# Moving the low parts of decoded weights and the division of the probabilities from GpSimd to VectorE

## The chip, the cores and the metric

The kernel runs on one core of one Trainium2 chip. The metric is the time of one execution on the device in microseconds (us). The profile comes from one execution of the same program under the hardware profiler. The core's engines work side by side, each through its own queue in order: TensorE (PE; PEld is its weight load), VectorE (DVE), ScalarE (ACT), GpSimd (POOL) and SyncE (SP), which here issues most of the DMAs.

## The reference, cut to what matters

Three layers follow each other on 2304 tokens of width 512.

```python
# 1. attention with a window of 64 keys: 4 batches, 8 heads, 576 positions, head width 64
scores = where(mask, scale * q @ k.T, -1e9)
attn = exp(scores - scores.max(-1))
attn = attn / (attn.sum(-1) + 1e-9)          # the division of the probabilities
x = attn @ v                                  # -> [2304, 512]
# 2. gated layer, w_a and w_b 512 x 1536, w_out 1536 x 512
x = ((x @ w_a) * (x @ w_b)) @ w_out
# 3. soft mixture of 8 experts with 4 slots each
logits = x @ phi                              # softmax over the tokens and over the slots
out = softmax(logits, 1) @ experts(softmax(logits, 0).T @ x)
```

The inputs are float32 for the attention and float64 for some weights: w_a, w_b and w_out arrive as pairs of 32-bit words, and the kernel makes float32 of them on the chip ("decoding").

## The kernel before, in words

The tokens are worked through in 18 tiles of 128. For each tile the attention is computed, then the products with w_a and w_b in three column groups (fg) of 512, then their product with w_out times phi, and running softmax sums. The products with w_a and w_b are made in two precisions: a weight is split into a high part, rounded to the fast matmul format, and a low part, the rest; each 128-deep step makes three matmuls (line 430): high x high, high x low, low x high.

All of w_a and w_b has to be decoded and split first: 24 pieces of 128x512, named by matrix, column group and depth, such as Da0.3 or Db2.1. One piece goes through seven steps: ScalarE takes the absolute value (line 365); VectorE clamps (367), shifts (369), sets the top bits (373) and the bottom bits (377); ScalarE rounds the high part (413); and the low part is the difference of the two (415). The difference is made by GpSimd. The decoded float32 piece lies in one of four buffers that are used in turn (tags gT0 and gT1), and a buffer is free for a later piece only when the difference is made. The 12 pieces of w_out (Po0 to Po11) go through the same decode steps in the same four buffers; their st buffers come from a pool of three, which late pieces of w_b use too, and they have no difference.

The attention of a tile has, on VectorE, the masking with its row extremes (line 271), the sums plus epsilon (290) and their reciprocal (292), and then the multiplication of the probabilities by it (296): in tiles 0 to 4 by GpSimd, in later tiles by VectorE. The transposes of the probabilities on TensorE wait for it.

The order of the work at the beginning is written out by hand: the string STARTUP is a list of steps, and the program advances the named piece of work by one step each time its name stands there. This fixes the order of every engine's queue and of the DMA issues (SyncE's, and GpSimd's for wo); an engine goes on to its next instruction as soon as that one's own inputs are there, so the queues may stand at different places of the list at the same time. Names are: Tq, Tv loads of q, k and v; Aq, Ak, As, An, Ap, Av the steps of the attention of a tile; Sa, Sb loads of a piece of w_a or w_b; Da, Db its seven steps; Ga, Gb the gated layer's matmuls of a tile and column group, with the copy (437) or product (439) at their end; Po a piece of w_out; Rt transposes; Ri constants; Ph the load of phi. Behind the list, only TensorE's order is written by hand.

Of the kernel before, what the change touches and what calls it, by code (L numbers as in the profile page):

```python
# [22 lines left out]
STARTUP = """
    Ak0 Tq0 Aq0 Tq0 Sb0.0 Aq0 Sa0.2 Db0.0 Ak0 Sb0.2 Db0.0 Ak0 As0 Da0.2 As0 Da0.2 Tq1 Db0.0 Db0.2 Db0.0 Tq1
    Sa0.0 Sa0.1 Aq1 As0 As0 Tq2 Db0.0 As0 Db0.0 Ak1 Da0.2 Db0.0 An0.0 An0.0 Ak1 Aq1 Ak1 As0 Da0.2 Db0.2 Db0.2
    As1 Db0.2 Da0.0 Db0.2 An0.1 As1 Ak2 Da0.2 Da0.0 An0.0 As1 Da0.0 Tq2 Db0.2 Da0.2 Da0.1 Sb0.1 Aq2 As1 Da0.2
    An0.1 Ap0.0 Da0.0 Da0.0 Sb0.3 Aq2 Tv0 Db0.1 Ak2 An0.1 Ap0.0 Da0.1 Db0.2 Ap0.1 Db0.3 Da0.0 An1.0 An1.0 Ak2
    Db0.1 Db0.1 Da0.1 As1 Tv0 Ap0.1 Av0 As1 Db0.1 Tq3 As2 Da0.1 Av0 Db0.1 As2 Da0.1 An1.1 An1.1 Db0.1 Ak3 Av0
    Db0.3 Sa0.3 Da0.1 As2 Da0.0 An1.0 Aq3 Da0.3 Tq3 Sa1.0 Gb0.0 Sa1.1 Da0.3 Ap1.0 An1.1 Da0.3 Tv1 Tv1 Aq3 Da0.1
    Ga0.0 Db0.3 As2 Da0.3 Ap1.0 Ak3 Db0.3 Ga0.0 Tq4 Ak3 Sb1.0 Ga0.0 Db0.1 Da0.3 Ap1.1 Da1.0 Da1.1 An2.0 As2 As3  # L30
    Db0.3 Da1.1 Da1.1 As3 Da0.3 Db0.3 Gb0.0 Da1.0 Ap1.1 Sa1.2 Av1 Sa1.3 Da0.3 As2 Da1.0 Av1 Gb0.0 Da1.1 An2.0
    Db0.3 Da1.0 An2.1 Da1.0 Ga0.0 Ga0.0 An2.1 Gb0.0 Da1.1 An2.0 Av1 Gb0.0 Tq4 Ap2.0 As3 Db1.0 Da1.0 Ga1.0 Aq4
    Gb1.0 Ak4 Po1 Da1.2 Db1.0 Ga1.0 Ga1.0 Da1.0 Ap2.0 Gb1.0 Db1.0 Da1.1 Tv2 Da1.3 Gb1.0 Da1.2 Ak4 As3 Sb1.1 Tv2
    Db1.0 Da1.1 Aq4 Da1.2 An2.1 Ak4 Ga1.0 Sb1.2 Da1.3 Da1.2 Db1.0 Da1.3 Sb1.3 Ga1.0 Da1.2 As3 Gb1.0 Da1.2 Da1.3
    Ap2.1 Po1 An3.0 Po1 Da1.2 Da1.3 Db1.0 Ga0.1 Db1.0 Po1 Ap2.1 As4 Ga0.1 Po4 Po1 Ga0.1 As4 Po1 Gb1.0 Da1.3
    Db1.1 As3 As4 Da1.3 Db1.2 Po1 An3.0 Db1.1 Db1.1 An3.0 Db1.2 Ga0.1 Tv3 Ga0.1 Db1.1 Po1 Po3 Db1.3 Db1.2 Po1
    Db1.1 Db1.1 Ph0 Db1.3 Db1.2 Av2 Gb0.1 Sa2.0 Sa2.1 Ga1.1 Av2 Po4 Ga1.1 Db1.2 Po4 Av2 An3.1 Po4 Db1.3 Ga1.1
    An3.1 Db1.3 Ga1.1 Db1.1 Ga1.1 Ap3.0 Db1.2 Tv3 Gb0.1 Ga2.0 Ga2.0 Ga2.0 As4 Db1.2 Po3 Ga2.0 As4 Da2.0 Ga2.0
    Po1 An3.1 Db1.3 Po3 Sa2.2 Po4 Ap3.1 An4.0 Db1.3 As4 Db1.3 Da2.0 Gb0.1 Ga2.1 Po3 An4.0 Po7 Po4 Po3 Ga2.1 Po3
    Po4 Ga2.1 Po3 Gb0.1 Gb0.1 Ap3.0 Po4 Ga2.1 Da2.1 Da2.1 Ap3.1 Da2.1 Av3 Gb2.0 Po3 Gb2.0 Da2.0 Po1 Tv4 Av3  # L40
    Da2.1 Sa2.3 Gb2.0 Gb2.0 Ri0 Tq5 Po1 Sb2.2 Ga2.1 Av3 Da2.0 Ga3.0 Da2.1 Da2.0 Po0 Ga3.0 Da2.2 Gb2.0 Da2.0
    Da2.2 An4.0 Po4 Po3 Gb1.1 Po1 Da2.0 Da2.2 Sb2.0 Gb1.1 Tv4 Da2.1 Gb1.1 Ga3.0 Po5 Da2.3 Da2.2 Po7 Ga3.0 Da2.2
    Po7 Da2.3 Gb1.1 Po7 Da2.2 Po4 An4.1 Tq5 Da2.1 Da2.2 Ga3.0 Po7 Da2.3 An4.1 Gb1.1 Po0 Da2.3 Po7 Ap4.0 Ga0.2
    Gb2.1 Po4 Ga0.2 Da2.3 Db2.0 Da2.3 Po4 Sb2.1 Db2.0 Po7 Da2.3 Po0 Ap4.0 Po5 Gb2.1 An4.1 Po4 Gb2.1 Gb2.1 Ga0.2
    Db2.0 Po0 Ga0.2 Po3 Po7 Po0 Db2.0 Po0 Ga0.2 Po6 Po5 Db2.0 Po5 Ga1.2 Po3 Ga1.2 Po3 Po5 Po7 Po5 Po0 Db2.1
    Gb2.1 Ga1.2 Po2 Db2.0 Po5 Db2.1 Po0 Po5 Po3 Db2.2 Db2.2 Db2.1 Po7 Po7 Gb3.0 Ga1.2 Db2.0 Ga1.2 Db2.2 Gb3.0
    Po2 Po7 Db2.1 Gb3.0 Po0 Db2.2 Ga3.1 Db2.1 Po5 Gb3.0 Po6 Ga3.1 Sb2.3 Po7 Po2 Gb3.0 Po5 Po5 Ga3.1 Db2.2 Po2
    Po6 Db2.1 Db2.2 Po2 Po2 Po6 Ga3.1 Ap4.1 Ga3.1 Db2.1 Po6 Po6 Po2 Db2.3 Gb3.1 Ga2.2 Po5 Gb3.1 Gb3.1 Po5 Po8
    Po0 Db2.2 Ak5 Gb3.1 Db2.3 Po9 Db2.3 Po0 Db2.3 Po0 Ak5 Ga2.2 Po6 Po0 Gb3.1 Ap4.1 Po8 Ga2.2 Po2 Ak5 Gb0.2
    Db2.3 Av4 Po8 Po8 Po8 Po2 Po2 Ga2.2 Po8 Db2.3 Gb0.2 Po11 Db2.3 Po2 Gb0.2 Po6 Tv5 Po2 Po10 Gb0.2 Ga2.2 Tv5  # L50
    Po2 Po8 Po9 Gb0.2 Po6 Ga3.2 Po6 Po11 Gb1.2 Po6 Ga3.2 Po9 Po8 Gb1.2 Ga3.2 Po6 Po11 Po9 Po8 Po10 Po10 Gb1.2
    Po9 Po6 Po8 Gb1.2 Rt0.0 Po9 Po8 Gb1.2 Ga3.2 Po9 Po9 Rt0.0 Aq5 Po9 Po8 Po11 Po10 Av4 Po11 Po8 Po11 Gb3.2
    Gb3.2 Aq5 Po11 Po10 Po9 Ga3.2 Po11 Po9 Po10 Po10 Gb3.2 Po11 Po10 Po9 Rt0.2 Po9 Po10 Gb3.2 Rt0.2 Rt0.1 Gb3.2
# [968 lines left out]
```

## Time and profile before

| what | value |
|---|---|
| median of 3 runs | 539.0 us (538.02 to 540.81) |
| the profiled execution, its own time | 537.18 us |
| its span, first to last instruction | 535.4 us |
| TensorE, share of the span | 92% |
| VectorE | 59% |
| ScalarE | 38% |
| GpSimd | 23% |
| HBM traffic | 215 GB/s over the span |
| mean granted TensorE clock | 0.991 of full speed |

The profiled execution is 1.8 us longer than its span (start and end around the first and last instruction). The shares are means over the whole span. The list STARTUP covers about the first 140 us.

### The profile page before, as it was taken

To read this page: it belongs to the slowest core of one execution; us is meant where nothing else is said; L and a number is where in the kernel's file an instruction comes from. 1 tells how busy PE (TensorE), PEld (TensorE's weight loads), DVE (VectorE), ACT (ScalarE), POOL (GpSimd) and SP (SyncE) were. 2 spreads that over 40 slices of the span, in tenths; PEclk is the share of its full clock that TensorE was granted. 3 is DMA by queue.
4 is the path that set the end of the run, shared out by engine and by line. 5 is a ranking of instruction groups with operands and counts; after the bars stand their busy time and mean duration, and the time that the engine had idled before them with its cause. 6 is when DMAs were issued, how large, how long until landed. Compare 5 with 4: busy or idle time off the path is not lost.

```text
span 535.4 us, 10977 instructions
## 1 busy us (share of the span) xinstructions
PE 492.5 (92%) x4039; PEld 362.4 (68%) x4039; DVE 315.1 (59%) x897; ACT 201.3 (38%) x621; POOL 120.7 (23%) x182
## 2 busy tenths in 40 slices
PE   4479788899998999999999999999999999989992
PEld 3367566677776777787778787787777777743452
DVE  3999999896456474756647466377674211242132
ACT  5667575354444232433324233243432212141012
POOL 3555447532000212112031120313221000020000
PEclk9998999999999999999999999999999999999997
DMA  9987168647444759776676657767779899799997
GB/s 275 259 240 240 44 224 249 204 146 203 119 119 104 199 129 239 192 184 156 159 190 145 179 142 174 197 159 180 190 213 291 305 360 366 265 343 341 348 350 245
DMA packets 142102, 116.01 MB, mean 217 GB/s; under 512 B 81888, under 2 KB 122848, under 8 KB 142048
## 3 DMA queue, kind: packets, MB, share of 16 engines
q1 hardware_dynamic: 136864, 99.58, 63.6%
q0 software_dynamic: 5184, 15.73, 10.4%
q8 instruction: 32, 0.52, 0.4%
q14 instruction: 22, 0.18, 0.1%
HBM read 90.90 MB, written 24.38 MB: 215 GB/s over the span
## 4 chain that ended last, share of the span: by engine, by line
PE 74%; DVE 15%; DMA 4%; issue 3%; ACT 1%; SPq 1%; POOL 0%; POOLq 0%; ACTq 0%
PE psb L430 25%; PE psa L430 24%; PE ops L924 3%; PE xps L346 3%; PE ups L558 3%; PE lps L482 3%; DVE w L373 3%; PE h L890 2%; PE s L258 2%; DVE w L377 2%; DVE w L367 2%; DVE pr L271 2%; PE tg L138 1%; DVE w L369 1%; DMA st<-in_moe_w_b_dram 1%
## 5 line engine op out<-in xcount | busy, mean ns | idle before, releaser
L430 PE MATMUL psb<-whb,x 128*128 128x512 f32 x432 | 153.7, 407 | 2.8 <-DVE g L439 2.2
L430 PE MATMUL psa<-wha,x 128*128 128x512 f32 x432 | 152.0, 406 | 2.4 <-ACT wha L413 1.6
L430 PEld LDWEIGHTS psb<-whb,x 128*128 128x128 f32 x432 | 81.3, 188 | 30.3 <-issue 9.9
L430 PEld LDWEIGHTS psa<-wha,x 128*128 128x128 f32 x432 | 81.1, 188 | 24.1 <-issue 3.9
L430 PE MATMUL psa<-wla,x 128*128 128x512 f32 x216 | 84.5, 391 | 1.0 <-POOL wla L415 1.0
L430 PE MATMUL psb<-wlb,x 128*128 128x512 f32 x216 | 84.6, 391 | 0.9 <-POOL wlb L415 0.9
L439 DVE TENSOR_TENSOR g<-psb,g 128x512 f32<-128x512 f32 x53 | 36.5, 689 | 71.5 <-PE psb L430 68.6
L437 ACT COPY g<-psa 128x512 f32<-128x512 f32 x53 | 31.1, 586 | 92.9 <-PE psa L430 82.6
L278 ACT ACTIVATE pr<-pr,nmx 128x128 f32<-128x128 f32 x144 | 56.0, 393 | 17.7 <-DVE nmx L271 17.7
L312 POOL DMA_DIRECT2D pd<-pq x48 | 26.4, 557 | 116.8 <-DVE pq L305 86.3
L430 PEld LDWEIGHTS psa<-wla,x 128*128 128x128 f32 x216 | 40.7, 189 | 8.3 <-POOL wla L415 1.4
L430 PEld LDWEIGHTS psb<-wlb,x 128*128 128x128 f32 x216 | 40.7, 189 | 7.6 <-POOL wlb L415 1.2
L349 ACT CAST x<-xps 128x512 fp32r<-128x512 f32 x18 | 10.6, 587 | 51.3 <-PE xps L346 51.3
L258 PE MATMUL s<-kTs,qTs 64*64 64x128 f32 x576 | 23.5, 299 | 6.4 <-DVE nmx L271 3.5
L457 DVE STREAM_TRANSPOSE gq<-g 128x512 f32<-128x512 f32 x39 | 27.4, 705 | 1.2 <-DMA gd<-gq 0.6
L278 ACT ACTIVATION_READ_ACCUMULATOR pr<-pr,nmx 128x1 f32 x144 | 27.4, 190 | 0.0
L318 POOL DMA_DIRECT2D pT<-pd x24 | 18.1, 758 | 39.9 <-DMA pd<-pq 35.4
L271 DVE CUSTOM_DVE_ANT_0 pr<-s,masks 128x128 f32<-128x128 f32 x112 | 24.8, 285 | 3.3 <-PE s L258 3.3
L258 PEld LDWEIGHTS s<-kTs,qTs 64*64 64x64 f32 x576 | 18.1, 147 | 10.1 <-issue 4.7
L232 POOL COPY kTs<-kTs 128x256 f32<-128x256 f32 x17 | 8.2, 483 | 66.1 <-DVE kTs L243 61.4
L415 POOL TENSOR_TENSOR wlb<-w,whb 128x512 fp32r<-128x512 f32 x12 | 17.5, 1455 | 18.4 <-ACT whb L413 18.4
L367 DVE TENSOR_SCALAR w<-w 128x512 f32<-128x512 f32 x24 | 14.4, 602 | 10.2 <-ACT w L365 10.2
(140 smaller groups left out, 721.8 us busy)
## 6 DMA issues: line engine op xcount, KB each, us to landing
xw<-in_moe_w_dram SPq DMA_DIRECT2D x39, 512.0 KB, 6.9
xw<-in_moe_w_dram SPq DMA_DIRECT2D x50, 256.0 KB, 5.9
gd<-gq SPq DMA_DIRECT2D x156, 64.0 KB, 2.9
gT<-gd SPq DMA_DIRECT2D x39, 256.0 KB, 3.2
st<-in_moe_w_b_dram SPq DMA_DIRECT2D x12, 512.0 KB, 5.9
st<-in_moe_w_a_dram SPq DMA_DIRECT2D x12, 512.0 KB, 5.5
st<-in_moe_w_out_dram SPq DMA_DIRECT2D x12, 512.0 KB, 5.2
pd<-pq POOLq DMA_DIRECT2D x48, 128.0 KB, 3.1
```

What stands on the lines that cost most here:

```text
L258: nc.tensor.matmul(sps[h][c, u], lhsT=qT[r, u, c], rhs=kTs[r, t % 2, u, W * b:W * b + P],)
L271: nc.vector.tensor_tensor_reduce(out=pr[:, u].rearrange("p (a k) -> p a k", a=2), in0=sps[h][:, u].rearrange("p (a k) -> p a k", a=2), in1 ...
L278: nc.scalar.activation(out=pr[:, u], in_=pr[:, u], func=ACTF.Exp, scale=-1.0, bias=nmx[:, i:i + 1], accum_out=sm[:, i:i + 1],)
L312: nc.gpsimd.dma_start(out=pd[:, :, i].rearrange("j k e -> k j e"), in_=pq[32 * i:32 * i + 32].rearrange("p j h u q -> p j (h u q)"),)
L318: nc.gpsimd.dma_start(out=pT, in_=pd[:, :, :, P * h:P * h + P].rearrange("j k i e -> (j k) i e"))
L346: nc.tensor.matmul(o, lhsT=vt[:, 2 * u + h, :], rhs=r)
L367: nc.vector.tensor_scalar(out=t, in0=t, scalar1=DBL_LO, scalar2=DBL_HI, op0=ALU.max, op1=ALU.min)
L415: nc.gpsimd.tensor_tensor(out=lo, in0=w32, in1=hi.bitcast(F32), op=ALU.subtract)
L430: nc.tensor.matmul(ps, lhsT=l[:, kk], rhs=r, start=(n == 0), stop=(n == 3 * KD - 1))
L437: nc.scalar.copy(out=pas[t, fg], in_=ps)
L439: nc.vector.tensor_tensor(out=g, in0=ps, in1=pas.pop((t, fg)), op=ALU.mult)
L457: nc.vector.transpose(out=gq.rearrange("p (j c t) -> p c j t", j=4, c=4), in_=gts[t][:, 512 * fg:512 * fg + 512].rearrange("p (c j f) -> p ...
```

## The change

Two edits of code, and a new order of the list. Line 415, the difference that makes the low part, is issued on VectorE for all 24 pieces. Line 296 is issued on VectorE for all tiles, so that the 10 multiplications of tiles 0 to 4 change their engine. In the list the seventh step of 23 of the 24 pieces stands 1 to 10 places later (Da0.1 keeps its place); the order of all other steps among themselves is the same.

```diff
 STARTUP = """
     Ak0 Tq0 Aq0 Tq0 Sb0.0 Aq0 Sa0.2 Db0.0 Ak0 Sb0.2 Db0.0 Ak0 As0 Da0.2 As0 Da0.2 Tq1 Db0.0 Db0.2 Db0.0 Tq1
-    Sa0.0 Sa0.1 Aq1 As0 As0 Tq2 Db0.0 As0 Db0.0 Ak1 Da0.2 Db0.0 An0.0 An0.0 Ak1 Aq1 Ak1 As0 Da0.2 Db0.2 Db0.2
-    As1 Db0.2 Da0.0 Db0.2 An0.1 As1 Ak2 Da0.2 Da0.0 An0.0 As1 Da0.0 Tq2 Db0.2 Da0.2 Da0.1 Sb0.1 Aq2 As1 Da0.2
-    An0.1 Ap0.0 Da0.0 Da0.0 Sb0.3 Aq2 Tv0 Db0.1 Ak2 An0.1 Ap0.0 Da0.1 Db0.2 Ap0.1 Db0.3 Da0.0 An1.0 An1.0 Ak2
+    Sa0.0 Sa0.1 Aq1 As0 As0 Tq2 Db0.0 As0 Db0.0 Ak1 Da0.2 An0.0 An0.0 Ak1 Aq1 Ak1 As0 Da0.2 Db0.0 Db0.2 Db0.2
+    As1 Db0.2 Da0.0 Db0.2 An0.1 As1 Ak2 Da0.2 Da0.0 An0.0 As1 Da0.0 Tq2 Db0.2 Da0.2 Da0.1 Sb0.1 Aq2 As1 An0.1
+    Ap0.0 Da0.0 Da0.0 Da0.2 Sb0.3 Aq2 Tv0 Db0.1 Ak2 An0.1 Ap0.0 Da0.1 Ap0.1 Db0.2 Db0.3 Da0.0 An1.0 An1.0 Ak2
     Db0.1 Db0.1 Da0.1 As1 Tv0 Ap0.1 Av0 As1 Db0.1 Tq3 As2 Da0.1 Av0 Db0.1 As2 Da0.1 An1.1 An1.1 Db0.1 Ak3 Av0
-    Db0.3 Sa0.3 Da0.1 As2 Da0.0 An1.0 Aq3 Da0.3 Tq3 Sa1.0 Gb0.0 Sa1.1 Da0.3 Ap1.0 An1.1 Da0.3 Tv1 Tv1 Aq3 Da0.1
+    Db0.3 Sa0.3 Da0.1 As2 An1.0 Aq3 Da0.0 Da0.3 Tq3 Sa1.0 Gb0.0 Sa1.1 Da0.3 Ap1.0 An1.1 Da0.3 Tv1 Tv1 Aq3 Da0.1
...
@@ att_n
         pr = st["pr"][hh]
-        eng = nc.gpsimd if t <= NFIRST else nc.vector
-        eng.tensor_tensor(out=pr, in0=pr, in1=rs.to_broadcast([P, 4, P]), op=ALU.mult)
+        nc.vector.tensor_tensor(out=pr, in0=pr, in1=rs.to_broadcast([P, 4, P]), op=ALU.mult)
@@ split_w
         nc.scalar.copy(out=hi, in_=w32)
         yield
-        nc.gpsimd.tensor_tensor(out=lo, in0=w32, in1=hi.bitcast(F32), op=ALU.subtract)
+        nc.vector.tensor_tensor(out=lo, in0=w32, in1=hi.bitcast(F32), op=ALU.subtract)
```

## Rows read from the trace of the kernel before

**Rows 1.** The page: busy us of each engine, and the span in 40 slices.

```profile
PE 492.5 (92%) x4039; PEld 362.4 (68%) x4039; DVE 315.1 (59%) x897; ACT 201.3 (38%) x621; POOL 120.7 (23%) x182
...
PE   4479788899998999999999999999999999989992
...
DVE  3999999896456474756647466377674211242132
```

**Rows 2.** The chain of waits, 8.9 to 113 us: start us, us, what.

```profile
8.91 0.04 DVE w L367
...
95.12 0.61 DVE wo L377
...
96.66 7.36 DMA st<-in_moe_w_b_dram
...
104.65 5.23 DMA st<-in_moe_w_out_dram
...
112.71 1.61 PE psa L430 x6
```

**Rows 3.** VectorE's groups, 8.9 to 95.73 us: busy us, mean ns, idle before.

```profile
L373 DVE SCALAR_TENSOR_TENSOR w<-st,w 128x512 int32<-128x512 int32 x20 | 17.4, 879 | 0.1
L377 DVE SCALAR_TENSOR_TENSOR w<-st,w 128x512 uint32<-128x512 uint32 x20 | 16.5, 833 | 0.1
L369 DVE TENSOR_SCALAR w<-w 128x512 int32<-128x512 int32 x20 | 14.1, 718 | 0.3
L367 DVE TENSOR_SCALAR w<-w 128x512 f32<-128x512 f32 x19 | 12.3, 649 | 0.9 <-ACT w L365 0.9
L290 DVE TENSOR_SCALAR rs<-sm 128x4 f32<-128x4 f32 x10 | 7.8, 783 | 0.0
...
L377 DVE SCALAR_TENSOR_TENSOR wo<-st,wo 128x512 uint32<-128x512 uint32 x4 | 3.7, 918 | 0.1
```

**Rows 4.** GpSimd's groups in the same stretch.

```profile
L415 POOL TENSOR_TENSOR wla<-w,wha 128x512 fp32r<-128x512 f32 x11 | 15.2, 1386 | 16.1 <-ACT wha L413 16.1
L415 POOL TENSOR_TENSOR wlb<-w,whb 128x512 fp32r<-128x512 f32 x8 | 11.7, 1464 | 11.2 <-ACT whb L413 11.2
L296 POOL TENSOR_TENSOR pr<-pr,rs 128x512 f32<-128x512 f32 x9 | 11.4, 1271 | 5.4 <-DVE rs L292 5.4
```

**Rows 5.** Timeline of VectorE and GpSimd, single instructions: start us, us, what.

```profile
18.05 0.16 DVE L290 TENSOR_SCALAR rs<-sm 128x4 f32<-128x4 f32 x1
...
39.02 1.27 POOL L415 TENSOR_TENSOR wla<-w,wha 128x512 fp32r<-128x512 f32 x1 [3.15 <-ACT wha L413]
...
39.12 1.71 DVE L377 SCALAR_TENSOR_TENSOR w<-st,w 128x512 uint32<-128x512 uint32 x1
...
52.49 0.42 DVE L369 TENSOR_SCALAR w<-w 128x512 int32<-128x512 int32 x1
...
53.16 0.68 DVE L373 SCALAR_TENSOR_TENSOR w<-st,w 128x512 int32<-128x512 int32 x1
53.76 0.68 DVE L377 SCALAR_TENSOR_TENSOR w<-st,w 128x512 uint32<-128x512 uint32 x1
54.36 0.41 DVE L369 TENSOR_SCALAR w<-w 128x512 int32<-128x512 int32 x1
```

**Rows 6.** Groups of the whole run: the multiplication of later tiles, on VectorE.

```profile
L296 DVE TENSOR_TENSOR pr<-pr,rs 128x512 f32<-128x512 f32 x26 | 17.9, 687 | 0.7
```

**Rows 7.** ScalarE's groups, 10 to 95 us.

```profile
L365 ACT ACTIVATE w<-st 128x512 f32<-128x512 f32 x19 | 12.7, 675 | 2.9 <-POOL wlb L415 1.8 <-DMA st<-in_moe_w_b_dram 0.7 <-POOL wla L415 0.3
...
L413 ACT CAST wha<-w 128x512 fp32r<-128x512 f32 x11 | 6.8, 619 | 9.2 <-DVE w L377 9.1
```

**Rows 8.** Timeline of VectorE, 97 to 124 us.

```profile
97.70 2.96 DVE L373 SCALAR_TENSOR_TENSOR wo<-st,wo 128x512 int32<-128x512 int32 x1
...
107.26 0.43 DVE L367 TENSOR_SCALAR w<-w 128x512 f32<-128x512 f32 x1 [1.74 <-ACT w L365]
...
114.20 1.52 DVE L369 TENSOR_SCALAR wo<-wo 128x512 int32<-128x512 int32 x1
115.76 2.06 DVE L373 SCALAR_TENSOR_TENSOR wo<-st,wo 128x512 int32<-128x512 int32 x1
...
122.98 1.65 DVE L373 SCALAR_TENSOR_TENSOR wo<-st,wo 128x512 int32<-128x512 int32 x1
```

**Rows 9.** Busy time of the engines in one window: length, PE, PEld, DVE, ACT, POOL, PEclk, DMA, GB/s.

```profile
60.00:110.00 50.00, 43.06 (x277) 32.22 (x278) 47.85 (x93) 28.38 (x72) 26.03 (x27) 1.00 0.65 202
```

More of the change, by code (lines that the diff above doesn't have):

```diff
@@ L28 @@
+    As1 Db0.2 Da0.0 Db0.2 An0.1 As1 Ak2 Da0.2 Da0.0 An0.0 As1 Da0.0 Tq2 Db0.2 Da0.2 Da0.1 Sb0.1 Aq2 As1 An0.1
+    Ap0.0 Da0.0 Da0.0 Da0.2 Sb0.3 Aq2 Tv0 Db0.1 Ak2 An0.1 Ap0.0 Da0.1 Ap0.1 Db0.2 Db0.3 Da0.0 An1.0 An1.0 Ak2
     Db0.1 Db0.1 Da0.1 As1 Tv0 Ap0.1 Av0 As1 Db0.1 Tq3 As2 Da0.1 Av0 Db0.1 As2 Da0.1 An1.1 An1.1 Db0.1 Ak3 Av0
-    Db0.3 Sa0.3 Da0.1 As2 Da0.0 An1.0 Aq3 Da0.3 Tq3 Sa1.0 Gb0.0 Sa1.1 Da0.3 Ap1.0 An1.1 Da0.3 Tv1 Tv1 Aq3 Da0.1
-    Ga0.0 Db0.3 As2 Da0.3 Ap1.0 Ak3 Db0.3 Ga0.0 Tq4 Ak3 Sb1.0 Ga0.0 Db0.1 Da0.3 Ap1.1 Da1.0 Da1.1 An2.0 As2 As3
@@ L31 @@
[L31 to L35, printed above, removed]
@@ L36 @@
-    Db1.1 As3 As4 Da1.3 Db1.2 Po1 An3.0 Db1.1 Db1.1 An3.0 Db1.2 Ga0.1 Tv3 Ga0.1 Db1.1 Po1 Po3 Db1.3 Db1.2 Po1
+    Db0.3 Sa0.3 Da0.1 As2 An1.0 Aq3 Da0.0 Da0.3 Tq3 Sa1.0 Gb0.0 Sa1.1 Da0.3 Ap1.0 An1.1 Da0.3 Tv1 Tv1 Aq3 Da0.1
+    Ga0.0 Db0.3 As2 Da0.3 Ap1.0 Ak3 Db0.3 Ga0.0 Tq4 Ak3 Sb1.0 Ga0.0 Da0.3 Ap1.1 Da1.0 Db0.1 Da1.1 An2.0 As2 As3
+    Db0.3 Da1.1 Da1.1 As3 Da0.3 Db0.3 Gb0.0 Da1.0 Ap1.1 Sa1.2 Av1 Sa1.3 As2 Da1.0 Av1 Gb0.0 Da1.1 An2.0 Da0.3
+    Da1.0 An2.1 Da1.0 Db0.3 Ga0.0 Ga0.0 An2.1 Gb0.0 Da1.1 An2.0 Av1 Gb0.0 Tq4 Ap2.0 As3 Db1.0 Da1.0 Ga1.0 Aq4
@@ L37 @@
+    Gb1.0 Ak4 Po1 Da1.2 Db1.0 Ga1.0 Ga1.0 Ap2.0 Gb1.0 Db1.0 Da1.1 Tv2 Da1.0 Da1.3 Gb1.0 Da1.2 Ak4 As3 Sb1.1 Tv2
+    Db1.0 Aq4 Da1.2 An2.1 Ak4 Ga1.0 Sb1.2 Da1.3 Da1.1 Da1.2 Db1.0 Da1.3 Sb1.3 Ga1.0 Da1.2 As3 Gb1.0 Da1.2 Da1.3
+    Ap2.1 Po1 An3.0 Po1 Da1.3 Db1.0 Da1.2 Ga0.1 Po1 Ap2.1 As4 Ga0.1 Po4 Po1 Ga0.1 As4 Po1 Db1.0 Gb1.0 Da1.3
+    Db1.1 As3 As4 Db1.2 Po1 An3.0 Db1.1 Db1.1 Da1.3 An3.0 Db1.2 Ga0.1 Tv3 Ga0.1 Db1.1 Po1 Po3 Db1.3 Db1.2 Po1
     Db1.1 Db1.1 Ph0 Db1.3 Db1.2 Av2 Gb0.1 Sa2.0 Sa2.1 Ga1.1 Av2 Po4 Ga1.1 Db1.2 Po4 Av2 An3.1 Po4 Db1.3 Ga1.1
-    An3.1 Db1.3 Ga1.1 Db1.1 Ga1.1 Ap3.0 Db1.2 Tv3 Gb0.1 Ga2.0 Ga2.0 Ga2.0 As4 Db1.2 Po3 Ga2.0 As4 Da2.0 Ga2.0
@@ L39 @@
-    Po1 An3.1 Db1.3 Po3 Sa2.2 Po4 Ap3.1 An4.0 Db1.3 As4 Db1.3 Da2.0 Gb0.1 Ga2.1 Po3 An4.0 Po7 Po4 Po3 Ga2.1 Po3
+    An3.1 Db1.3 Ga1.1 Ga1.1 Ap3.0 Db1.2 Tv3 Db1.1 Gb0.1 Ga2.0 Ga2.0 Ga2.0 As4 Po3 Ga2.0 As4 Db1.2 Da2.0 Ga2.0
+    Po1 An3.1 Db1.3 Po3 Sa2.2 Po4 Ap3.1 An4.0 Db1.3 As4 Da2.0 Db1.3 Gb0.1 Ga2.1 Po3 An4.0 Po7 Po4 Po3 Ga2.1 Po3
     Po4 Ga2.1 Po3 Gb0.1 Gb0.1 Ap3.0 Po4 Ga2.1 Da2.1 Da2.1 Ap3.1 Da2.1 Av3 Gb2.0 Po3 Gb2.0 Da2.0 Po1 Tv4 Av3
     Da2.1 Sa2.3 Gb2.0 Gb2.0 Ri0 Tq5 Po1 Sb2.2 Ga2.1 Av3 Da2.0 Ga3.0 Da2.1 Da2.0 Po0 Ga3.0 Da2.2 Gb2.0 Da2.0
-    Da2.2 An4.0 Po4 Po3 Gb1.1 Po1 Da2.0 Da2.2 Sb2.0 Gb1.1 Tv4 Da2.1 Gb1.1 Ga3.0 Po5 Da2.3 Da2.2 Po7 Ga3.0 Da2.2
@@ L43 @@
-    Po7 Da2.3 Gb1.1 Po7 Da2.2 Po4 An4.1 Tq5 Da2.1 Da2.2 Ga3.0 Po7 Da2.3 An4.1 Gb1.1 Po0 Da2.3 Po7 Ap4.0 Ga0.2
-    Gb2.1 Po4 Ga0.2 Da2.3 Db2.0 Da2.3 Po4 Sb2.1 Db2.0 Po7 Da2.3 Po0 Ap4.0 Po5 Gb2.1 An4.1 Po4 Gb2.1 Gb2.1 Ga0.2
+    Da2.2 An4.0 Po4 Po3 Gb1.1 Po1 Da2.2 Sb2.0 Gb1.1 Tv4 Da2.1 Gb1.1 Ga3.0 Po5 Da2.3 Da2.2 Da2.0 Po7 Ga3.0 Da2.2
+    Po7 Da2.3 Gb1.1 Po7 Da2.2 Po4 An4.1 Tq5 Ga3.0 Po7 Da2.3 An4.1 Da2.1 Da2.2 Gb1.1 Po0 Da2.3 Po7 Ap4.0 Ga0.2
+    Gb2.1 Po4 Ga0.2 Da2.3 Db2.0 Da2.3 Po4 Sb2.1 Db2.0 Po7 Po0 Ap4.0 Da2.3 Po5 Gb2.1 An4.1 Po4 Gb2.1 Gb2.1 Ga0.2
@@ L45 @@
     Db2.0 Po0 Ga0.2 Po3 Po7 Po0 Db2.0 Po0 Ga0.2 Po6 Po5 Db2.0 Po5 Ga1.2 Po3 Ga1.2 Po3 Po5 Po7 Po5 Po0 Db2.1
-    Gb2.1 Ga1.2 Po2 Db2.0 Po5 Db2.1 Po0 Po5 Po3 Db2.2 Db2.2 Db2.1 Po7 Po7 Gb3.0 Ga1.2 Db2.0 Ga1.2 Db2.2 Gb3.0
+    Gb2.1 Ga1.2 Po2 Db2.0 Po5 Db2.1 Po0 Po5 Po3 Db2.2 Db2.2 Db2.1 Po7 Po7 Gb3.0 Ga1.2 Ga1.2 Db2.2 Gb3.0 Db2.0
     Po2 Po7 Db2.1 Gb3.0 Po0 Db2.2 Ga3.1 Db2.1 Po5 Gb3.0 Po6 Ga3.1 Sb2.3 Po7 Po2 Gb3.0 Po5 Po5 Ga3.1 Db2.2 Po2
-    Po6 Db2.1 Db2.2 Po2 Po2 Po6 Ga3.1 Ap4.1 Ga3.1 Db2.1 Po6 Po6 Po2 Db2.3 Gb3.1 Ga2.2 Po5 Gb3.1 Gb3.1 Po5 Po8
@@ L49 @@
-    Po0 Db2.2 Ak5 Gb3.1 Db2.3 Po9 Db2.3 Po0 Db2.3 Po0 Ak5 Ga2.2 Po6 Po0 Gb3.1 Ap4.1 Po8 Ga2.2 Po2 Ak5 Gb0.2
-    Db2.3 Av4 Po8 Po8 Po8 Po2 Po2 Ga2.2 Po8 Db2.3 Gb0.2 Po11 Db2.3 Po2 Gb0.2 Po6 Tv5 Po2 Po10 Gb0.2 Ga2.2 Tv5
+    Po6 Db2.1 Db2.2 Po2 Po2 Po6 Ga3.1 Ap4.1 Ga3.1 Po6 Po6 Po2 Db2.1 Db2.3 Gb3.1 Ga2.2 Po5 Gb3.1 Gb3.1 Po5 Po8
+    Po0 Ak5 Gb3.1 Db2.3 Po9 Db2.3 Po0 Db2.3 Db2.2 Po0 Ak5 Ga2.2 Po6 Po0 Gb3.1 Ap4.1 Po8 Ga2.2 Po2 Ak5 Gb0.2
+    Db2.3 Av4 Po8 Po8 Po8 Po2 Po2 Ga2.2 Po8 Db2.3 Gb0.2 Po11 Po2 Db2.3 Gb0.2 Po6 Tv5 Po2 Po10 Gb0.2 Ga2.2 Tv5
```

## The prediction

> **What bounds the kernel now.** I read the page first: busy times, then the slices [rows 1]. TensorE is busy for 92% of the span, but its first ten slices (13.4 us each) are the thin ones, and in the same slices VectorE stands at nine tenths or full; after them VectorE falls to a half. So the change, which touches only instructions of the hand-ordered list (about 0 to 140 us), lies in the one stretch where VectorE and not TensorE is full. Next I read the chain of waits through that stretch [rows 2]. From 8.91 us to the end of the instruction that starts at 95.12 us it has practically nothing but VectorE, with short issue times between. Then it passes, through SyncE's queue, to the load of a piece of w_b that starts at 96.66 us and takes 7.36 us, to a w_out load, and from 112.71 us it is TensorE. What VectorE's queue saves before 95.73 us thus moves these loads, and with them TensorE's start on its solid stretch, earlier by the same amount, as long as TensorE can be ready too. Last I read the groups of VectorE and GpSimd in just this stretch, 8.9 to 95.73 us [rows 3, 4], and a few single instructions [rows 5] to see why VectorE is full.
>
> Those groups are the point. A decode step has two durations: the undisturbed one, 0.42 us for a `tensor_scalar` and 0.68 us for the or-steps of lines 373 and 377, and a long one [rows 5]. The or-step that starts at 39.12 us lasts 1.71 us; a GpSimd subtraction had started at 39.02 us and ran 1.27 us, and the or-step ends about half a microsecond after it. The `tensor_scalar` of line 290, with only 4 columns, takes 0.16 us undisturbed and 0.78 us in the mean of ten [rows 3]. VectorE is held while GpSimd reads the same memory, and the held time is counted as busy.
>
> **What the change removes.** In 8.9 to 95.73 us GpSimd runs 11 + 8 subtractions and 9 multiplications, 38.3 us in all [rows 4]. The time by which they hold VectorE is count x (mean - undisturbed) over the groups [rows 3, 5]: line 373 20 x (0.879 - 0.68) = 4.0; line 377 20 x (0.833 - 0.68) = 3.1, and for wo 4 x (0.918 - 0.68) = 0.9; line 369 20 x (0.718 - 0.42) = 6.0; line 367 19 x (0.649 - 0.42) = 4.3; line 290 10 x (0.783 - 0.16) = 6.2. Together 24.5 us. I count all of it as removed: the other GpSimd work of this stretch (copies of kTs, the build of ri, DMA issues) is short and stays.
> Not all of the 38.3 us is held time: part of a GpSimd instruction passes while VectorE runs something that is not held, such as the reduces of line 271, or ends what it had begun. From above, the gain is bounded by the whole 38.3 us; that is a rival below.
> The Trainium skill, "SBUF — State Buffer", Who interferes with whom, says that the two engines share a pair of ports as an exclusive lock: whichever comes first keeps it for its whole instruction, the other fully blocks. If VectorE always wanted that pair, all 38.3 us would come back, against 24.5 by the groups; I go by the groups.
>
> **What it adds.** 24 subtractions and 10 multiplications on VectorE, 128x512, two operands in SBUF. VectorE already runs that multiplication later in the kernel, at 0.69 us [rows 6], and two or-steps of the same shape start 0.60 us apart (53.16, 53.76, then the next at 54.36) although each is listed with 0.68 us [rows 5]: neighbours overlap by 0.08 us. I take 0.60; the bounds are 0.60 and 0.69. By the new list's order 28 of the 34 stand ahead of the chain's handover at 95.12 us, so 28 x 0.60 = 16.8 us (19.3 at the upper bound).
> The Trainium skill, "VectorE: DVE Perf Modes", The DRAIN you can't avoid, says that the next VectorE instruction does not start until the pipe is empty; that would charge the full 0.69 and shrink the gain by 2.5 us. The starts in the row say otherwise.
>
> **What it moves.** Each subtraction now stands in VectorE's queue and needs the rounded high part that ScalarE copies after line 377, so everything behind it (the next decode steps, the masks' reduces, the products of line 439) would wait for ScalarE. The copy takes 0.62 us [rows 7]. I counted VectorE's work in the new list between line 377 of a piece and its subtraction, at 0.34 us for a `tensor_scalar` and 0.60 for the wide ones: 0.7 us for Da2.3, 1.4 to 2.7 for six others, more than 3 for the remaining 17. That is what moving them "a few pieces later" buys, so I put this wait at nothing; its cover is that other VectorE work, and without it each would cost some 0.65 us.
> A second wait is real. A decode buffer (four in turn) is free only when its subtraction is done, and then ScalarE's `abs` of a later piece (0.67 us, [rows 7]) must run before VectorE's line 367 of that piece. In the new list Da0.3 has no VectorE work between the two and Po7 has 0.6 us: 0.75 + 0.15 = 0.9 us of new waits before 95 us. Db2.3 has the same, but behind the handover.
> The multiplications keep their place in the list, right behind or a few pieces behind the reciprocal on the same queue: no new wait there. TensorE gets some of them later than GpSimd delivered them, first of all An0.0, but TensorE is at about half in that part of the list [rows 1]. GpSimd's queue loses its two long kinds, so its copies and the DMA issues of wo can only come earlier; no DMA is added, and SyncE's queue keeps its order.
>
> **The sum.** 24.5 - 16.8 - 0.9 = 6.8 us earlier at the handover. The profiled execution took 537.18 us (span 535.4), which gives 530.4; the median of the runs, 539.0, lies 1.8 us above that execution, which gives 532.2. I write 531.5 us, between the two. Bounds of this case: with 0.69 instead of 0.60 the gain is 24.5 - 19.3 - 0.9 = 4.3 us. At the other end, four instructions behind the handover are held too [rows 8]: 2.3 (97.70 us), 1.1 (114.20), 1.4 (115.76) and 1.0 (122.98), 5.8 us against 6 more instructions of 0.60 = 3.6. If VectorE still sets the pace there and the new waits cost nothing, the gain is 24.5 + 5.8 - 16.8 - 3.6 = 9.9 us, or 527.3.
>
> **Rivals.**
> *TensorE cannot follow.* Between 60 and 110 us it is already busy for 43.06 of 50 us [rows 9], 6.9 us idle, as much as the sum wants to save, and a matmul listed as busy may also wait inside. It must come to 112.71 us as much earlier as the loads do. If it makes up only a third of that idle time, the gain is 2.3 us: 534.9 on the profiled execution, 536.7 on the median. For it: a queue in order, whose inputs come from three engines. Against it: TensorE is far from full before 60 us [rows 1], and much of its idle time is waiting for what VectorE decodes.
> *VectorE waits for ScalarE: slower.* If ScalarE is late, the subtractions become waits at the head of VectorE's queue. Each of the 19 before 95 us would cost about one copy's 0.65 us: 12.4 us, so 537.2 - 6.8 + 12.4 = 542.8. It decides from a mean wait of 6.8 / 19 = 0.36 us. For it: GpSimd spent 16.1 + 11.2 us waiting for these copies [rows 4], and ScalarE also runs the exponentials. Against it: the 0.7 to 9 us of other work in between, and ScalarE itself sat waiting for VectorE's line 377 [rows 7].
> *More comes back than the means show.* With all 38.3 us the time is 537.2 - (38.3 - 16.8 - 0.9) = 516.6 us. Against it: the groups' excess [rows 3] has no room for it, and TensorE's 6.9 idle us [rows 9] would not do.
> *The holds are not GpSimd's doing.* Then nothing comes back and 16.8 + 0.9 are added: 554.9 us. The fit of starts and ends [rows 5] speaks against it.
>
> **How the numbers follow.** Half a per cent, 2.7 us, is about what these runs can tell from no change. My forecast (gain 4.3 to 8 us) 0.64; VectorE still the bound behind the handover (up to 10 us) 0.04; more comes back 0.01; TensorE cannot follow 0.17, of which 0.05 still passes 2.7 us; VectorE waits for ScalarE 0.11; holds not GpSimd's doing 0.03. So faster 0.74, within the bound 0.12, slower 0.14. The range 527 to 538 takes in the first two cases and nearly all of the case in which TensorE cannot follow; the forecast's own is 529 to 534.5.
>
> **What would show it.** Right: over 8.9 to 95 us the means of lines 367, 369, 373, 377 and 290 fall to 0.42, 0.42, 0.68, 0.68 and 0.16 us; lines 415 and 296 appear on VectorE at about 0.69; its first idle time behind that shows at about 99 us, where it now stands at 105.5 to 107.26 [rows 8]; the w_b load starts near 90 us. Wrong: idle time of VectorE before line 415, released by ScalarE's line 413; or the same VectorE times with TensorE's idle time between 60 and 105 us undiminished.

## The result and the profile after

| what | before | after |
|---|---|---|
| median of the runs | 539.0 us (538.02 to 540.81, 5 runs) | 534.56 us (534.13 to 536.23, 5 runs) |
| the profiled execution, its own time | 537.18 us | 534.13 us |
| its span | 535.4 us | 532.4 us |
| mean granted TensorE clock | 0.991 | 0.986 |

The ratio is 0.9916, with a 95% interval of 0.9889 to 0.9944: 4.4 us faster. The two profiled executions differ by 3.05 us, the spans by 3.0 us. The other 1.4 us is only that the execution profiled of before lies 1.8 us under its median and the one of after 0.4 us.

In the kernel after, the lines behind 295 of the kernel before have numbers one lower (296 is 295, 415 is 414, 439 is 438). First the page of after: busy time of each engine, the span in 40 slices and the granted clock in the same slices.

```profile
PE 493.6 (93%) x4039; PEld 364.3 (68%) x4039; DVE 306.8 (58%) x931; ACT 200.8 (38%) x621; POOL 74.2 (14%) x148
...
PE   4579699999989999999999999999999999989992
...
PEclk9998799999999999999999999999999999999998
```

Against [rows 1], GpSimd lost 46.5 us of work and VectorE, with 34 instructions more, is 8.3 us less busy. TensorE's slices from the sixth to the eighth are fuller, 9 tenths and not 8, and behind them little differs. Its fifth (53 to 67 us) is thinner than its neighbours, 6 tenths, and there the clock is at 7 tenths. VectorE's groups of the same stretch as in [rows 3] (busy us, mean ns of one, idle before them):

```profile
L372 DVE SCALAR_TENSOR_TENSOR w<-st,w 128x512 int32<-128x512 int32 x20 | 13.6, 689 | 0.1
L376 DVE SCALAR_TENSOR_TENSOR w<-st,w 128x512 uint32<-128x512 uint32 x20 | 13.6, 688 | 0.1
L368 DVE TENSOR_SCALAR w<-w 128x512 int32<-128x512 int32 x20 | 8.7, 441 | 0.2
L366 DVE TENSOR_SCALAR w<-w 128x512 f32<-128x512 f32 x20 | 8.6, 430 | 2.1 <-ACT w L364 2.1
L414 DVE TENSOR_TENSOR wla<-w,wha 128x512 fp32r<-128x512 f32 x12 | 8.1, 680 | 0.0
L295 DVE TENSOR_TENSOR pr<-pr,rs 128x512 f32<-128x512 f32 x10 | 6.8, 684 | 0.0
...
L414 DVE TENSOR_TENSOR wlb<-w,whb 128x512 fp32r<-128x512 f32 x8 | 5.5, 684 | 0.3 <-ACT whb L412 0.3
...
L290 DVE TENSOR_SCALAR rs<-sm 128x4 f32<-128x4 f32 x10 | 1.8, 183 | 0.0
```

The means of [rows 3] are down to about the undisturbed values, line 290 from 783 to 183 ns, and VectorE waits only 0.3 us for the rounded high part. Of the 2.1 us before line 366, 1.29 stand at the first step of the stretch, before any subtraction; 0.78 are a new wait:

```profile
9.64 0.43 DVE L366 TENSOR_SCALAR w<-w 128x512 f32<-128x512 f32 x1 [1.29 <-ACT w L364]
...
33.06 0.43 DVE L366 TENSOR_SCALAR w<-w 128x512 f32<-128x512 f32 x1 [0.78 <-ACT w L364]
```

That first step stands at 8.91 us in [rows 2]. In after the w_a load in front of it took 6.29 us and not 5.57. In the other runs the same step stands anywhere from 8.54 us (experiment 6) to 10.06 us (experiment 2), so these 0.7 us need not come from the change. The chain of waits of after, 61 to 113 us (start us, us, what):

```profile
61.70 0.61 DVE wla L414
...
62.35 1.22 PE psa L429 x2
63.58 0.85 PE two L138 x4
64.43 1.91 PE xps L345 x32
66.34 1.25 PE psb L429 x3
...
70.79 0.69 PE psb L429 x3
...
78.61 0.44 PE two L138 x4
79.05 0.70 PE psa L429 x3
79.75 1.08 PE xps L345 x32
...
84.27 0.04 DVE g L438
...
92.93 0.61 DVE wo L376
...
94.47 6.37 DMA st<-in_moe_w_b_dram
...
101.51 5.30 DMA st<-in_moe_w_out_dram
...
109.67 1.61 PE psa L429 x6
```

The end of this chain answers to [rows 2]: the handover came from 95.73 to 93.54 us (92.93 + 0.61), the w_b load took 6.37 us and not 7.36, the w_out load starts 3.14 us earlier, and TensorE's row of 112.71 us stands at 109.67, 3.04 us earlier. That is the whole change of the span. But the middle is new: from 62.35 to 84.27 us the chain is TensorE, where before it was VectorE. (From 38.96 to 49.80 us the chain of after also runs through TensorE and a w_b load, but VectorE has no idle time there.)

Single instructions of after at the place where the chain changes engines (in brackets the idle time in front of an instruction and what ended it):

```profile
59.32 0.68 DVE L438 TENSOR_TENSOR g<-psb,g 128x512 f32<-128x512 f32 x1
...
61.62 0.68 DVE L414 TENSOR_TENSOR wla<-w,wha 128x512 fp32r<-128x512 f32 x1
62.22 0.69 DVE L295 TENSOR_TENSOR pr<-pr,rs 128x512 f32<-128x512 f32 x1
...
62.35 0.79 PE L429 MATMUL psa<-wla,x 128*128 128x512 f32 x1 [3.53 <-DVE wla L414]
...
63.61 0.59 ACT L436 COPY g<-psa 128x512 f32<-128x512 f32 x1 [1.41 <-PE psa L429]
...
67.56 0.43 DVE L366 TENSOR_SCALAR wo<-wo 128x512 f32<-128x512 f32 x1 [1.00 <-ACT wo L364]
```

The same place in the kernel before, which [rows 5] do not reach:

```profile
60.74 0.49 PE L430 MATMUL psa<-wha,x 128*128 128x512 f32 x1 [1.63 <-ACT wha L413]
62.28 0.50 PE L430 MATMUL psa<-wla,x 128*128 128x512 f32 x1 [1.04 <-POOL wla L415]
...
62.70 0.68 DVE L439 TENSOR_TENSOR g<-psb,g 128x512 f32<-128x512 f32 x1
...
85.00 0.68 DVE L439 TENSOR_TENSOR g<-psb,g 128x512 f32<-128x512 f32 x1
```

The products of 62.70 and 85.00 us are those of 59.32 and 84.27 us in after. TensorE's matmul with the low part of Da1.3 starts at 62.28 us before and at 62.35 us after. In after TensorE stood idle for 3.53 us until it came. VectorE made that part at 61.62 us, by its place in the list, behind the product of 59.32 us, the masks, a reciprocal and two decode steps. From there the delay runs in a circle: TensorE is late, ScalarE waits 1.41 us for TensorE's result (and 0.62 us more at 66.38 us), and VectorE waits 1.00 us for ScalarE. Two windows of after, with the columns of [rows 9], show the second part of it:

```profile
60.00:110.00 50.00, 45.12 (x290) 35.19 (x291) 45.64 (x107) 29.60 (x77) 6.70 (x13) 0.93 0.65 202
60.00:70.00 10.00, 7.64 (x53) 6.26 (x54) 8.90 (x28) 5.50 (x16) 0.00 (x0) 0.66 0.43 121
```

The granted clock was 1.00 over 60 to 110 us in [rows 9] and is 0.93 now, 0.66 in the first ten microseconds: from 60.26 to 67.08 us it stood at the lower of its two levels (1.2 and not 2.4 GHz).

### The profile page after: what moved, and what is told of

Read it like the earlier page. It is cut to its first block, busy times and chain, and to the rows that moved or that the text cites. A ratio compares the mean times of both kernels' runs of the same rounds, so it can differ in the third digit from the quotient of the medians.

```text
span 532.4 us, 10963 instructions
## 1 busy us (share of the span) xinstructions
PE 493.6 (93%) x4039; PEld 364.3 (68%) x4039; DVE 306.8 (58%) x931; ACT 200.8 (38%) x621; POOL 74.2 (14%) x148
## 3 DMA queue, kind: packets, MB, share of 16 engines
q0 software_dynamic: 5184, 15.73, 10.4%
## 4 chain that ended last, share of the span: by engine, by line
PE 79%; DVE 10%; DMA 5%; issue 2%; ACT 2%; SPq 1%; POOL 0%; POOLq 0%; ACTq 0%
PE psb L429 27%; PE psa L429 26%; PE xps L345 4%; PE ops L923 3%; PE lps L481 3%; PE s L258 3%; PE ups L557 3%; PE h L889 2%; DMA st<-in_moe_w_b_dram 2%; PE tg L138 1%; DVE w L372 1%; DMA st<-in_moe_w_a_dram 1%; DVE pr L271 1%; PE tk L138 1%; DMA st<-in_moe_w_out_dram 1%
## 5 line engine op out<-in xcount | busy, mean ns | idle before, releaser
L295 DVE TENSOR_TENSOR pr<-pr,rs 128x512 f32<-128x512 f32 x36 | 24.7, 686 | 0.7
L232 POOL COPY kTs<-kTs 128x256 f32<-128x256 f32 x17 | 9.4, 553 | 92.2 <-DVE kTs L243 63.8
L364 ACT ACTIVATE w<-st 128x512 f32<-128x512 f32 x24 | 16.1, 672 | 14.4 <-DVE wlb L414 5.8
```

What stands on the lines that cost most here:

```text
L295: nc.vector.tensor_tensor(out=pr, in0=pr, in1=rs.to_broadcast([P, 4, P]), op=ALU.mult)
```

## The experiments

Theory A, as I held it once I had seen the result: the held time came back as worked out, but between 60 and 85 us TensorE did not follow, because it waited for low parts that VectorE makes late in its list. Against it stood two rivals: that the gain comes from the new order of the list and not from the engines, and that the holds are not GpSimd's doing. The kernel before had a median of 539.14 us beside experiments 1 to 4, 538.97 us beside 5 to 7 and 538.8 us beside 8.

**1. Da1.3's low part earlier.** The kernel after, with the last two steps of Da1.3 moved ahead.

```diff
-Ap2.1 As4 Ga0.1 Po4 Po1 Ga0.1 As4 Po1 Db1.0 Gb1.0 Da1.3 Db1.1 ... An3.0 Db1.1 Db1.1 Da1.3 An3.0
+Ap2.1 As4 Ga0.1 Po4 Da1.3 Da1.3 Po1 Ga0.1 As4 Po1 Db1.0 Gb1.0 Db1.1 ... An3.0 Db1.1 Db1.1 An3.0
```

> The changed kernel with one list edit: the last two steps of piece Da1.3 (rounding, subtraction) stand 10 to 15 places earlier, so that VectorE makes this low part right behind line 368 of Po1 (about 57.3 us) and not at 61.62 us. Theory A: in the changed kernel TensorE has become the bound from 62 to 84 us, because it stood 3.53 us (58.8 to 62.35) waiting for this one low part, and then ran at half the granted clock until 67 us. Then that wait falls below 1 us, the clock stays at its upper level there, the w_b load that started at 94.47 us starts at 91 to 93 us, and the time is 530.5 to 533 us, against 534.6. Rival B: VectorE's queue alone sets the handover and the wait of TensorE lies beside it: the load starts at 94 to 95 us and the time stays at 534 to 535.5.

Measured: 536.65 us (12 runs, 534.52 to 538.69), 0.9955 [0.9935, 0.9974]: 2.1 us more than after, not less. A row of TensorE's timeline, a window and a row of the chain of this kernel:

```profile
68.86 0.50 PE L428 MATMUL psb<-wlb,x 128*128 128x512 f32 x1 [3.67 <-DVE wlb L413]
```

```profile
70.00:80.00 10.00, 10.00 (x65) 7.58 (x65) 7.41 (x17) 5.01 (x15) 2.00 (x5) 0.84 0.19 75
```

```profile
110.04 2.16 PE psa L428 x6
```

The wait did not go, it moved 6.5 us on, to the next late low part (Db1.1's), with the same length. The clock fell again, at 69.88 us and once more at 110.84 us, where the row of 1.61 us in after takes 2.16. So the expectation failed: one wait was taken away and the next in the list took its place. That explains a time no better than after, not a worse one. At the product of 84.27 us this kernel still stands 0.3 us ahead (83.96), and at the row of 109.67 us it stands 0.4 us behind (110.04); most of the 1.7 us by which its span is longer arises right behind that, while the clock is low (110.84 to 114.25 us). Whether A holds was open until the late parts went together (experiment 5).

**2. Both edits of engine, the list of before.**

```diff
@@ the kernel before
-        eng = nc.gpsimd if t <= NFIRST else nc.vector
-        eng.tensor_tensor(out=pr, in0=pr, in1=rs.to_broadcast([P, 4, P]), op=ALU.mult)
+        nc.vector.tensor_tensor(out=pr, in0=pr, in1=rs.to_broadcast([P, 4, P]), op=ALU.mult)
-        nc.gpsimd.tensor_tensor(out=lo, in0=w32, in1=hi.bitcast(F32), op=ALU.subtract)
+        nc.vector.tensor_tensor(out=lo, in0=w32, in1=hi.bitcast(F32), op=ALU.subtract)
```

> Both engine edits with the list of before, so that each subtraction stands where GpSimd's stood. VectorE's own work between line 376 of a piece and its subtraction is then 0.3 us for Da2.3 and over 1 us for the other 23, against 0.65 us that ScalarE's copy takes. Theory A (the wait of TensorE for a late low part counts): Da1.3's low part comes some 0.9 us earlier than in the changed kernel, so 533 to 534.6 us, no slower than the changed kernel. Rival C (the later places are what makes the change pay, since without them VectorE waits for ScalarE): idle time of VectorE before line 414 of several us, and 536 to 539 us.

Measured: 533.21 us (4 runs, 532.9 to 533.95), 0.9893 [0.9863, 0.9923]. It is no slower than after; the intervals of the two overlap. VectorE waits 1.3 us for high parts where after waits 0.3, and TensorE still stands 3.3 us for one low part. Moving the low parts later is therefore not what pays; the engines are. (The new list with the engines of before was not run.)

**3. Only the multiplication on VectorE.** The kernel before with the first of the two edits above.

> The kernel before with only the multiplication of tiles 0 to 4 on VectorE; subtractions and list as before. If the gain is held time returned less work added, this part gives about nothing: 10 multiplications hold VectorE for some 6 to 7 us (their GpSimd time is 12.5 us, and the holds are about half to two thirds of it) and add 10 x 0.60 = 6.0: 538 to 539.5 us. Rival: every instruction moved brings the same share of the gain of 4.4 us, 10 of 34: 537.7 us. Rival: TensorE gets the probabilities later and loses: above 540 us.

Measured: 536.97 us (10 runs, 535.95 to 538.83), 0.9969 [0.9951, 0.9988]: 2.2 us faster by the medians, more than expected. Its groups over 8.9 to 95.73 us, where [rows 3] has 879 and 783 ns:

```profile
L372 DVE SCALAR_TENSOR_TENSOR w<-st,w 128x512 int32<-128x512 int32 x20 | 15.9, 802 | 0.1
...
L290 DVE TENSOR_SCALAR rs<-sm 128x4 f32<-128x4 f32 x10 | 7.0, 698 | 0.0
```

Counted as in the prediction over all groups, 18.4 of the 24.5 us of held time stay. So 6.1 us come back for 9 x 0.60 = 5.4 added, a gain of 0.7. The measured one is 1.5 us larger, but the interval of the ratio reaches from 0.6 to 2.6 us, so this excess is not clear of noise. The profiled execution, 538.83 us, is the longest of its ten and cannot show more. The rival in which TensorE loses by later probabilities (above 540 us) did not come.

**4. Only the low parts on VectorE.** The kernel after with the multiplications of tiles 0 to 4 given back to GpSimd (the first edit undone).

> The changed kernel with the multiplication of tiles 0 to 4 back on GpSimd. The subtractions' part of held time is 18 us of the 24.5 in the stretch before 95.7 us, against 19 x 0.60 = 11.4 added, so nearly the whole gain is theirs: 533.5 to 535.5 us, and VectorE's line 290 or 366 shows ten long instances again. Rival: by count, 24 of 34 of the gain of 4.4 us, 3.1 us: 535.9 us.

Measured: 537.63 us (10 runs, 535.97 to 539.84), 0.9974 [0.9954, 0.9995]: 1.5 us faster than before by the medians, less than expected. A group of VectorE in the same stretch and a row of TensorE's timeline:

```profile
L373 DVE SCALAR_TENSOR_TENSOR w<-st,w 128x512 int32<-128x512 int32 x20 | 15.3, 773 | 0.1
```

```profile
62.23 0.79 PE L430 MATMUL psa<-wla,x 128*128 128x512 f32 x1 [4.26 <-DVE wla L415]
```

By the same count 8.0 us of held time stay, so 16.5 come back for 20 x 0.60 = 12.0: 4.5 us. Of it 1.5 reaches the median, and the interval of the ratio ends at 2.5. The long instances are not in line 290, as the expectation had it (179 ns in the mean), but in the decode steps and the subtractions. TensorE stands 4.26 us at the place where it stood 3.53 in after, and the clock is at its lower level at 60.7 to 67.5 us and at two later places. That the waits cost the difference is argued from these rows, not shown by this run.

**5. Four late steps earlier.** The kernel after with the edit of experiment 1, and the low parts of Db1.1 and Db1.2 and the multiplication An3.1 moved as well.

```diff
-Ga1.1 Db1.2 Po4 Av2 ... Ga1.1 Ga1.1 Ap3.0 Db1.2 Tv3 Db1.1 Gb0.1 ... As4 Db1.2 Da2.0 Ga2.0 Po1 An3.1 Db1.3
+Ga1.1 Db1.1 Db1.2 Po4 Av2 ... Ga1.1 Ga1.1 Ap3.0 Db1.2 Db1.2 An3.1 Tv3 Gb0.1 ... As4 Da2.0 Ga2.0 Po1 Db1.3
```

> The changed kernel with four low steps earlier in the list: Da1.3 as in the run before, and Db1.1, Db1.2 and the multiplication An3.1 each a few places earlier, right behind the copy they need. In the run with Da1.3 alone TensorE's wait of 3.5 us went from that piece to the next one it needs, Db1.1 (3.67 us, at 64.7 to 68.86 us), so that it stood where it stood before at 84 us. Theory A (TensorE bounds 56 to 84 us through late low parts): with both out of the way VectorE's line for Gb2.0, at 84.27 us in the changed kernel, starts at 80 to 82.5 us, the w_b load behind it 1 to 3 us earlier than 94.47, and the time is 530.5 to 534 us. Rival B (another input of TensorE, or VectorE's own queue, takes over at once): 84 us and 94 us stay, and the time is 534.5 to 537 us.

Measured: 532.08 us (6 runs, 531.22 to 534.11), 0.9883 [0.9861, 0.9905], span 529.4 us. Its window of 60 to 110 us, and rows of its chain:

```profile
60.00:110.00 50.00, 45.68 (x290) 34.30 (x286) 46.91 (x110) 29.31 (x70) 8.82 (x15) 1.00 0.71 214
```

```profile
80.63 0.68 DVE g L437
...
89.29 0.62 DVE wo L375
...
90.83 6.50 DMA st<-in_moe_w_b_dram
...
97.87 5.89 DMA st<-in_moe_w_out_dram
...
106.62 1.61 PE psa L428 x6
```

Here the 3.5 us wait is gone, the clock is 1.00, and the chain from 56 to 89.91 us is practically all VectorE again. The handover is 5.8 us ahead of before (95.73) and TensorE's row 6.09 us ahead (112.71), as is the span (535.4 - 529.4 = 6.0). This is the course that the prediction's sum describes, 1.0 us short of its 6.8, and A is borne out: it was the late steps that kept TensorE back. Experiment 1 took only the first of them.

**6. GpSimd reads on, for nobody.** The kernel after; beside each subtraction GpSimd makes one of its own, of the high part from itself, into a buffer for which nobody waits. It adds work and changes none of the computation.

```diff
         nc.vector.tensor_tensor(out=lo, in0=w32, in1=hi.bitcast(F32), op=ALU.subtract)
+        nc.gpsimd.tensor_tensor(
+            out=cst.rearrange("p t s -> p (t s)")[:, 0:512], in0=hi.bitcast(F32), in1=hi.bitcast(F32), op=ALU.subtract
+        )
```

> The changed kernel, and beside each of VectorE's 24 subtractions GpSimd subtracts as well, the high part from itself, 128x512, into a table that is written over later; nobody waits for it. If GpSimd's reading is what held VectorE, the decode steps get their long instances back (means of 0.6 to 0.85 us for lines 366 to 376, 0.18 us falling to nothing in none of them, line 290 near 0.7 us), some 18 us of held time in the stretch before 95 us come on top of the added subtractions, and the time is 545 to 553 us. Rival (the long instances came from the waits and the order around GpSimd's results, not from its reading): means stay at 0.43 and 0.69 us and the time at 534 to 536 us.

Measured: 546.23 us (4 runs, 545.1 to 547.99), 1.0144 [1.0118, 1.017], 11.7 us more than after. Groups of VectorE, then of GpSimd, over 8.9 to 95.73 us:

```profile
L414 DVE TENSOR_TENSOR wla<-w,wha 128x512 fp32r<-128x512 f32 x9 | 7.8, 867 | 0.0
...
L290 DVE TENSOR_SCALAR rs<-sm 128x4 f32<-128x4 f32 x9 | 3.1, 346 | 0.0
```

```profile
L415 POOL TENSOR_TENSOR cst<-wha 128x512 f32<-128x512 f32 x10 | 11.7, 1166 | 29.2 <-ACT wha L412 29.2
L415 POOL TENSOR_TENSOR cst<-whb 128x512 f32<-128x512 f32 x8 | 10.0, 1245 | 16.3 <-ACT whb L412 16.1
```

Means that stood at 680 and 183 ns in after are at 867 and 346. Nothing waits for these subtractions, so the longer VectorE instructions come from GpSimd's running beside them. That refutes the rival that the holds are something else. The time lies in the range expected, but the holds are smaller than expected: line 290 has 346 ns and not near 700, lines 366 and 368 have 474 and 488, and the held time is about 10 us and not 18. Counted from the first step of the stretch (8.54 us here), the instruction of 92.84 us in after comes 9.5 us later (101.25), which is about this held time.
The Trainium skill, "SBUF — State Buffer", Who interferes with whom, calls the port pair that the two engines share a lock, which one of them holds for its whole instruction. The rows agree in kind. In amount, VectorE lost about 10.4 us against the means of after for these 21.7 us of GpSimd, and 24.5 for 38.3 in [rows 3, 4]: about half and two thirds, not all.

**7. Both edits of engine, the list of before, the same four steps earlier.** Experiment 2 with the steps of experiment 5 moved.

> Both engine edits with the list of before (533.2 us in its run), and the same four steps earlier as in the run with four. Theory A: as there, TensorE loses its waits for Da1.3 and Db1.1, and the time is 529.5 to 533 us, the fastest of all. Rival B: another wait takes their place, 533 to 535 us.

Measured: 530.66 us (5 runs, 530.18 to 531.53), 0.9851 [0.983, 0.9872], span 529.7 us. It is the fastest kernel of this study. The row of its chain that answers to 112.71 us before and 106.62 in experiment 5:

```profile
107.02 1.61 PE psa L428 x6
```

Its TensorE waits for low parts only 0.6 us in all over the list (0.4 and 0.2), and the granted clock over 60 to 110 us is 1.00. Against experiment 5 the intervals touch, so between the two lists no order is shown.

**8. The four steps earlier, engines as before.** The kernel of experiment 7 with both operations given back to GpSimd.

> The kernel before with the same four steps moved earlier in the list (Da1.3's last two, Db1.1's and Db1.2's low parts, the multiplication An3.1) and both edits of engine left out: GpSimd keeps the low parts and the multiplications of tiles 0 to 4. Theory A (before 95 us VectorE, held by GpSimd, is the bound, and TensorE's wait at 62 us is covered by it): the earlier steps alone give nothing, 537 to 541 us against 539, and VectorE's means over 8.9 to 95.73 us stay those of before. Rival E (the earlier steps pay by themselves, whichever engine does the work): as much as they gave with VectorE's low parts, 2.5 us, so 535 to 537 us.

Measured: 539.94 us (10 runs, 538.1 to 542.92), 1.0022 [0.9998, 1.0045]. A group of VectorE in the same stretch:

```profile
L372 DVE SCALAR_TENSOR_TENSOR w<-st,w 128x512 int32<-128x512 int32 x20 | 17.4, 879 | 0.1
```

The mean is that of [rows 3]. Other lines differ (367's steps have 741 ns and not 649, 290's 568 and not 783), but the count over all groups gives 25.4 us of held time, where before has 24.5, and the time is that of before. So these four earlier steps alone give nothing. With one and the same list, experiments 7 and 8 differ by 9.3 us: that is what the two engine edits are worth in it. Not all of it need be held time: over 60 to 70 us the granted clock is 0.66 in the profiled execution of experiment 8, which at 542.58 us is 2.6 us above its median.

## Why the prediction was right, and where it was off

*The time.* 534.56 us lies in the range of 527 to 538 and on the side forecast as likeliest. It is 3.1 us above the 531.5 predicted and just above the forecast's own 529 to 534.5: a gain of 4.4 us where the sum had 6.8. The range held because it was wide enough for the rival "TensorE cannot follow", not because the sum was met.

*What is removed: right.* Of the 24.5 us of held time 1.2 are left by the same count (20 x (0.009 + 0.008 + 0.021 + 0.010) + 10 x 0.023 for line 290), so 23.3 came back. Experiments 6 and 8 show that the holds come from GpSimd's running beside VectorE. That all 38.3 us would return did not happen.

*What is added: right.* The subtractions are listed with 0.68 us and start 0.60 apart (61.62 and 62.22).
The Trainium skill, "VectorE: DVE Perf Modes", The DRAIN you can't avoid, says that the next instruction waits until the pipe is empty, which would charge the full 0.68, but it adds that one that is not held starts earlier. These starts, as those in [rows 5], agree with the addition, which the prediction left out.

*The new waits: right in kind and nearly in size.* The sum had 0.9 us before line 367 (366 in after). One wait of this kind came, 0.78 us at 33.06 us, forecast at 0.75. The rest of the 2.1 us that line 366 waits in after is the 1.29 us at the first step, where [rows 3] has 0.9 us. The rival in which VectorE waits for ScalarE's high parts did not come: 0.3 us in all.

*The pass-through: this step failed.* "What VectorE's queue saves before 95.73 us thus moves these loads ... as long as TensorE can be ready too" carries a condition, and the sum let it hold. VectorE was ahead by 3.4 us at the product of 62.70 us (59.32 in after), and only by 0.7 at that of 85.00 (84.27). From there to the handover it took 9.27 us and not 10.73, so that the handover came 2.2 us earlier. The w_b load, which the prediction put near 90 us, started at 94.47, and VectorE's first idle time behind the handover ended at 104.04 us and not near 99. The w_b load, shorter by 1.0 us, gave the rest of the 3.0.

The sum can be redone for the three stretches between the first step, the two products and the handover: held time gone (counted as in the prediction, over each stretch), less 0.60 us for each instruction added, less the wait of 0.78 us. For the first stretch this gives 16.4 - 0.8 - 18 x 0.60 - 0.8 = 4.0 us, and VectorE gained 4.1. For the third it gives 4.0 - 4 x 0.60 = 1.6, and 1.5 came. For the second it gives 5.1 - 0.4 - 7 x 0.60 = 0.5, and VectorE lost 2.7. So of these 6.1 us 3.2 were lost in the one stretch in which TensorE is the chain, and 0.7 to the later first step; 2.2 reached the handover.

In the terms of the prediction the rival "TensorE cannot follow" took a part of the forecast gain, which fell short by 2.4 of 6.8 us by the medians, 3.8 by the profiled executions. I had weighed TensorE's idle time between 60 and 110 us as a sum of 6.9 us [rows 9], and not asked which instruction it waits for: the low part of Da1.3 was made by GpSimd and let TensorE start at 62.28 us before, and by VectorE it comes at the same time, 62.35, because it stands behind other work in VectorE's queue. The prediction's own sign of this, TensorE's idle time undiminished, is nearly there: in the window of 50 us TensorE is busy for 45.12 us and not 43.06, but by the estimate of the last section 2.6 us of that are the lower clock. Without that wait and the next ones (experiment 5) the same engine edits give 5.8 us at the handover and 6.0 in the span, inside the sum's bounds of 4.3 and 9.9. Counted from the first step, the stretch to the handover is 2.9 us shorter than before in after, 5.7 in experiment 5 and 6.8 in experiment 7 (9.94 to 89.99 us). Experiments 7 and 8 put the edits at 9.3 us, inside these bounds too.

*What stays open.* The parts done alone gave 2.2 and 1.5 us (experiments 3 and 4) where the count has 0.7 and 4.5. For the second, TensorE's wait of 4.26 us and the clock are likely reasons, argued and not tried; the first may be noise.

## What to carry to other kernels

When an engine is relieved, don't only sum what it saves: go through the next engine's waits in that stretch, instruction by instruction, and ask which of its inputs the relieved engine now makes and how far back in its queue it makes them. Two engines that slow each other are best told by means per group against the undisturbed duration; such a sum came out to within about a microsecond here, once nothing else stood in the way. And where one wait is removed and the time does not follow, look for the next one of the same kind before the theory is dropped.
